# Who fetches the first token tiles, who splits the first expert's weights, and in which order the SyncE queue sees them

## The chip, the core and the metric

One NeuronCore of a Trainium2 chip runs the whole program in one launch. The metric is the device time of one execution in microseconds (us); lower is better. TensorE (PE, with its weight loads PEld), VectorE (DVE), ScalarE (ACT) and GpSimd (POOL) each run their own instruction stream in order. SyncE (SP) computes nothing: it issues DMAs, also in order, and reads a table entry into a register before a DMA whose address is only known at run time. POOL also issues DMAs, the indirect ones, whose row numbers lie in SBUF.

## The reference, cut to what matters

```python
# q, k, v: (8, 8, 576, 64) float32; 4608 tokens of 512 numbers come out of the attention
scores = scale * (q_c @ k_c.T)               # in chunks of 64 tokens, per batch and head
attn   = exp(scores - max); attn /= attn.sum(-1) + 1e-9
x      = (attn @ v_c)                        # -> (4608, 512)

logits     = norm(x) @ norm(expert_emb).T / tau       # 8 experts
expert_idx = argmax(logits);  gate_w = softmax(logits)[expert_idx]
for e in range(8):                                    # top-1 mixture, w1 (8,512,1024), w2 (8,1024,512)
    out[mask_e] = gate_w * (relu(x[mask_e] @ w1[e]) @ w2[e])

h = out @ w_in                                        # (512, 2048)
y = (h * sigmoid(1.702 * h)) @ w_out                  # (2048, 512)
```

## The kernel before, in words

The work has three stages. **Attention**: 36 tiles of 128 tokens (NTILE), one loop step `n` per tile plus three steps of tail. A step handles several tiles at different depths: scores of tile n (`emit_S`), probabilities of n-1, the product with V of n-2, and for tile n-3 `emit_X` (line 401), which makes a two-part f16 copy `xr` of the token rows (high part by DVE, low part by two POOL instructions, lines 417 and 418, for tiles below 33), and stores it to the DRAM table `xs`. `emit_XT` transposes `xr` on TensorE two to five steps later, ACT copies it out (`evac_XT`, line 437), and `emit_L` forms the router's logits.

**Routing**: after each batch of tiles the generator `gate` (line 504) works out on DVE, a few instructions at a time (`drip`, `steps`), each token's expert, weight and position; `place` (line 492) then scatters a tile's records into the DRAM tables `mtab[0]` and `mtab[1]` by an indirect POOL DMA. These wait in a list `scats` and are issued one or two a step by `scat`. After 24 tiles (NPART) the expert with most tokens is known; its first three tiles (NSURE) are taken from these 24, so that they can start before the attention ends. `first_load` (line 802) brings that expert's weights in eight SyncE DMAs of 512 KB, one a step from n = 31; `first_split` (line 813) cuts them into two f16 parts, sixteen pieces c = 0 to 15, two a step: ACT makes the high part, and the low part is made by DVE (one instruction) for even c and by POOL (two instructions, lines 788 and 789) for odd c. After the last batch, `tables` (line 642) works out where all later tiles lie (`idx_g`) and which expert weights come next.

**Mixture**: each tile i goes through `find(i)` (line 848: the tile's 128 records out of both halves of `mtab`; an indirect POOL DMA for i < 3, a SyncE DMA at a row read into a register for later ones), `fetch(i)` (line 860: POOL adds the halves and gathers the token rows from `xs` by an indirect DMA into `xg`, two buffers), `turn(i)` (line 876: a transposing SyncE DMA into `xTm`, two buffers), `mm1(i)` (line 893, 96 matmuls), and `mm2(i)` (line 926, 24 matmuls, then an evacuation that ends in a SyncE store to `ys`). mm1 of the first two tiles and the rest of the routing are interleaved by hand at lines 1049 to 1090. Then the next expert's weights are loaded (`load_next`, four DMAs of 1 MB), three blocks of the last stage's weights (`big_load`, 512 KB each) follow, and the loop at line 1266 runs over tiles 3 to 38: mm1(i), turn(i+2), fetch(i+3), find(i+4), a conditional swap of weights, mm2(i-1).

The last stage, a dense feed-forward network, starts when the loop ends and is not touched.

Of the kernel before, what the change touches and what calls it, by code (L numbers as in the profile page):

```python
# [17 lines left out]
ENG = mybir.EngineType  # L18
# [16 lines left out]
def kernel(  # L35
# [13 lines left out]
    nc = tc.nc  # L49
    B, H, S, D = q.shape  # L50
    NT, DM = out.shape
    NE = emb.shape[0]
# [451 lines left out]
    def gate(bi):  # L504
        t0, n = batches[bi]
        T = slice(t0, t0 + n)
        lg = lg_t.pop(bi)
        dl = small("dl", n, w=NE)
        nc.vector.tensor_copy(dl, lg[:, 0:n, NE:2 * NE])
        yield  # L510
        l = small("l", n, w=NE)
        nc.vector.tensor_tensor(out=l, in0=lg[:, 0:n, 0:NE], in1=dl, op=ALU.add)
        yield
        nc.vector.tensor_tensor(
            out=l, in0=l, in1=rn_all[:, T].unsqueeze(2).to_broadcast([128, n, NE]), op=ALU.mult
        )
        yield
        mx = small("mx", n)
        nc.vector.tensor_reduce(out=mx.unsqueeze(2), in_=l, axis=AX.X, op=ALU.max)
        yield  # L520
        nc.vector.tensor_tensor(
            out=l, in0=l, in1=mx.unsqueeze(2).to_broadcast([128, n, NE]), op=ALU.subtract
        )
        yield
        w = small("w", n, w=NE)
        nc.vector.scalar_tensor_tensor(
            out=w, in0=l, scalar=0.0, in1=io_re.unsqueeze(1).to_broadcast([128, n, NE]),
            op0=ALU.is_ge, op1=ALU.mult,
        )
        yield  # L530
        mw = small("mw", n)
        nc.vector.tensor_reduce(out=mw.unsqueeze(2), in_=w, axis=AX.X, op=ALU.max)
        yield
        oh = att.tile([128, 8, NE], F16, tag="g_oh", name="g_oh", bufs=2)[:, 0:n]
        nc.vector.tensor_tensor(
            out=oh, in0=w, in1=mw.unsqueeze(2).to_broadcast([128, n, NE]), op=ALU.is_equal
        )
        yield
        ex = small("ex", n, w=NE)
        nc.scalar.activation(out=ex, in_=l, func=AF.Exp)  # L540
        yield "pe"
        rkf = gb[:, 128:128 + n * NE]
        rk = rkf.rearrange("p (a e) -> p a e", a=n)
        ohf = oh.rearrange("p a e -> p (a e)")
        nc.tensor.matmul(rkf, tri16, ohf, start=True, stop=False)
        for j in range(1, n):
            nc.tensor.matmul(rkf[:, j * NE:], ones16, ohf[:, 0:(n - j) * NE], start=False, stop=False)
        nc.tensor.matmul(
            rk, ones16, cum.unsqueeze(1).to_broadcast([128, n, NE]), start=False, stop=True
        )  # L550
        sm = small("sm", NE)
        nc.vector.tensor_reduce(
            out=sm.unsqueeze(2), in_=oh.rearrange("p a e -> p e a"), axis=AX.X, op=ALU.add
        )
        yield
        nc.vector.tensor_tensor(out=cum, in0=cum, in1=sm, op=ALU.add)
        yield
        last = totals("cnt") if t0 + n in (NPART, NTILE) else None
        se = small("se", n)
        nc.vector.tensor_reduce(out=se.unsqueeze(2), in_=ex, axis=AX.X, op=ALU.add)  # L560
        yield
        nc.vector.tensor_scalar(se, se, 1e-9, None, op0=ALU.add)
        yield
        nc.vector.reciprocal(out=se, in_=se)
        yield
        nc.vector.scalar_tensor_tensor(
            out=meta[:, T, 0], in0=se, scalar=2.0 ** (-2 * W_EXP), in1=is_all[:, T],
            op0=ALU.mult, op1=ALU.mult,
        )
        yield  # L570
        po = small("po", n, w=NE)
        nc.vector.tensor_tensor(out=po, in0=rk, in1=oh, op=ALU.mult)
        yield
        pf = small("pf", n)
        nc.vector.tensor_reduce(out=pf.unsqueeze(2), in_=po, axis=AX.X, op=ALU.add)
        yield
        nc.vector.tensor_copy(pi_all[:, T], pf)
        yield
        scats.extend((now[0], lambda t=t: place(t)) for t in range(t0, t0 + n))
        if t0 + n == NPART:  # L580
            yield from order(last)
            first_weights()
            scats.extend((now[0], lambda i=i: find(i)) for i in range(NSURE))
            scats.extend((now[0], lambda i=i: fetch(i)) for i in range(2))
        if t0 + n == NTILE:
            yield from tables(last)

# [173 lines left out]
    def reg(ap, engines, hi):  # L761
        return nc.values_load(ap, engines=engines, min_val=0, max_val=hi)
# [50 lines left out]
    def first_split(n):  # L813
        for _ in range(n):
            c = fs_n[0]
            fs_n[0] += 1
            w_split(c // 8 + 1, c % 8, 512, (nc.vector, nc.gpsimd)[c % 2])

    flag = {}

# [26 lines left out]

    def find(i):
        mt_t[i] = [mo.tile([128, 2], F32, tag=f"mt{a}", name=f"mt{a}", bufs=6) for a in range(2)]
        row = reg(idx_g[0:1, i:i + 1], [ENG.SP], NE * NT - 128) if NSURE <= i < SURE else None  # L850
        for a in range(2):
            if row is not None:
                nc.sync.dma_start(out=mt_t[i][a][:, :], in_=mtab[a][bass.ds(row, 128), :])
                continue
            nc.gpsimd.indirect_dma_start(
                out=mt_t[i][a][:, :], out_offset=None, in_=mtab[a][:, :],
                in_offset=bass.IndirectOffsetOnAxis(ap=idx_g[:, i:i + 1], axis=0),
            )

    def fetch(i):  # L860
        mt, other = mt_t[i]
        nc.gpsimd.tensor_tensor(
            out=mt.bitcast(I32), in0=mt.bitcast(I32), in1=other.bitcast(I32), op=ALU.add
        )
        mt_t[i] = mt
        xg = mo.tile([128, 2 * DM], F16, tag="xg", name="xg", bufs=2)
        src = xs[0:NPART * 128, :] if i < NSURE else xs[:, :]
        nc.gpsimd.indirect_dma_start(
            out=xg[:, :], out_offset=None, in_=src,
            in_offset=bass.IndirectOffsetOnAxis(ap=mt_t[i].bitcast(I32)[:, 1:2], axis=0),  # L870
        )
        xg_t[i] = xg

    def turn(i):
        xT = mo.tile([128, 2 * KD, 128], F16, tag="xTm", name="xTm", bufs=2)
        nc.sync.dma_start_transpose(xT, xg_t.pop(i))
        xTm_t[i] = xT
# [34 lines left out]
    def mm2(i):  # L912
        mm2_part(i, 0, KF)
        mm2_evac(i)
# [89 lines left out]
    for n in range(NTILE + 3):  # L1004
        now[0] = n
        u, step = n // QR + 1, n % QR
        ev = [[], []]
        if u < NQ:
            ev = emit_T(u, "ku" if step == 0 else "qu")
            if step == 1 and u + 2 < NQ:  # L1010
                load_qk(u + 2)
        for f in ev[0]:
            f()
        on(n - 3, emit_sq)
        for f in ev[1]:
            f()
        turned = []
        if n - 1 in back:
            evac_XT(back[n - 1])
            turned.append(back[n - 1])  # L1020
        scat()
        drip(1)
        if n in front:
            emit_XT(front[n])
        on(n, emit_S, max_S)
        if n in front:
            evac_XT(front[n])
            turned.append(front[n])
        drip(1)
        on(n - 3, end_X)  # L1030
        drip(1)
        on(n - 1, emit_PT, evac_PT)
        on(n - 2, emit_PV)
        issue_v(v_due(n))
        if len(scats) > (4 if n < 30 else 0):
            scat()
        on(n, exp_S)
        drip(1)
        on(n - 2, emit_x)
        drip(1)  # L1040
        if n in back:
            emit_XT(back[n])
        for t in sorted(turned):
            end_L(t)
        if n >= NTILE - 5 and fl_n[0] < 8:
            while not first:
                drip(1)
            first_load()
        if n >= NTILE - 3:
            first_split(2)  # L1050
        if n == NTILE - 2:
            turn(0)
        if n == NTILE - 1:
            turn(1)
            fetch(2)
        if n >= NTILE:
            drip(6)
            mm1_part(0, n - NTILE)
# [19 lines left out]
        scat()  # L1078
    mm1_part(1, 3)
    steps(99)  # L1080
    find(3)
    mm2(0)
    mm1(2)
    fetch(3)
    turn(3)
    find(4)
    while todo:
        steps(1)
    fetch(4)
    att_stack.close()  # L1090


# [31 lines left out]
    def big_split():  # L1124
# [123 lines left out]
        run(99)  # L1248
        write()

    load_next(NSURE - 1, 1)
    load_next(NSURE - 1, 2)
    find(5)
    swap(NSURE, 1)
    mm2(1)
    turn(4)
    fetch(5)
    find(6)
    for b in range(NRAW):
        big_load(b)  # L1260
# [5 lines left out]
    for i in range(NSURE, SURE):  # L1266
# [6 lines left out]
            find(i + 4)  # L1273
        if i + 1 < SURE:
            swap(i + 1, 1)
        mm2_part(i - 1, 0, KF)
        swap(i, 2)
        mm2_evac(i - 1)
        if i < LASTD:
            next(dec, None)  # L1280
        if i == LASTD:
# [404 lines left out]
```

## Time and profile before

| What | Value |
|---|---|
| median of 3 executions | 1436.17 us (1432.81 to 1441.11) |
| the profiled execution | 1442.98 us, of which span 1441.2 us |
| TensorE busy | 1263.9 us (88% of the span) |
| VectorE, ScalarE, GpSimd busy | 1034.0 (72%), 721.1 (50%), 759.7 us (53%) |
| attention, TensorE's last score product | starts at 220.35 us |
| first mixture matmul | 240.48 us |
| mixture ends, last stage begins | about 720 us |

The span is cut into stages by the lines that run in it. A timeline row gives the start, the duration, the engine, the source line, what is written and read, and how often; brackets at its end hold the idle time ahead of it and what ended that idle time. Shares of busy time over the whole span say little here, since the change touches only the passage from attention to mixture, some 125 us long.

### The profile page before, as it was taken

The numbers are of one execution on the slowest core, as the hardware profiler recorded it, in microseconds if no ns is written. First come the engines' busy times: TensorE is split into PE (matmuls) and PEld (weight loads), VectorE is DVE, ScalarE is ACT, GpSimd is POOL, SyncE is SP. The second block draws the span as 40 slices with busy tenths as digits, with TensorE's granted clock in tenths as the row PEclk, the third lists the DMA queues.
The fourth block names the chain that finished last, engine by engine and source line by source line (L and its number), as shares of the span: only waits on it lengthen the run. The fifth ranks groups of instructions, "written<-read, shape, count | busy, mean of one in ns | idle before, by whom it ended". The sixth has DMA issues, their size and how long they took to land. (4 is left out here: it accounts for less than half of the span.)

```text
span 1441.2 us, 35556 instructions
## 1 busy us (share of the span) xinstructions
PE 1263.9 (88%) x14098; PEld 1043.1 (72%) x14098; DVE 1034.0 (72%) x1888; ACT 721.1 (50%) x1285; POOL 759.7 (53%) x676
## 2 busy tenths in 40 slices
PE   6767664779999999999879999998989999999995
PEld 4656553556766666676568888887878888888885
DVE  3868786826776668876568687877769696968681
ACT  6967653214453535553445464545454544545451
POOL 1445548413344344445037666666657575757663
PEclk8987975989999999999979999999999999999998
DMA  9888875175886768896604435351606262534412
GB/s 208 221 169 181 161 125 147 46 226 135 231 219 125 200 155 220 258 258 189 199 9 118 147 89 176 69 188 37 220 16 190 75 170 95 133 131 117 147 60 88
DMA packets 231224, 214.33 MB, mean 149 GB/s; under 512 B 139064, under 2 KB 184120, under 8 KB 231040
## 3 DMA queue, kind: packets, MB, share of 16 engines
q1 hardware_dynamic: 216304, 184.84, 49.8%
q0 software_dynamic: 7344, 19.71, 4.3%
q10 hardware_dynamic: 7392, 7.36, 1.6%
q8 instruction: 112, 1.84, 0.6%
q14 instruction: 72, 0.59, 0.2%
HBM read 155.06 MB, written 37.14 MB: 133 GB/s over the span
## 5 line engine op out<-in xcount | busy, mean ns | idle before, releaser
L1426 PEld LDWEIGHTS <-wS 128*128 128x128 f16 x3024 | 299.4, 99 | 73.1 <-issue 35.4
L893 PE MATMUL ph<-xTm,w1HL 128*128 128x128 f16 x3744 | 230.1, 225 | 35.5 <-DMA xTm<-xg 13.3
L893 PEld LDWEIGHTS <-w1HL 128*128 128x128 f16 x3744 | 222.6, 101 | 50.8 <-issue 14.9
L926 PE MATMUL py<-w2HL,hT 128*128 128x512 f16 x936 | 208.2, 379 | 0.0
L926 PEld LDWEIGHTS <-hT 128*128 128x128 f16 x936 | 90.1, 98 | 101.4
L1426 PEld LDWEIGHTS <-w2HL 128*128 128x128 f16 x864 | 84.5, 98 | 10.6
L1426 PEld LDWEIGHTS <-w1HL 128*128 128x128 f16 x864 | 84.6, 98 | 9.8
L1131 POOL TENSOR_TENSOR wS<-d_f,wS 128x512 f16<-128x512 f32 x28 | 35.9, 1283 | 95.0 <-ACT wS L1130 95.0
L1572 POOL DMA_INDIRECT out_dram<-hT,idc x36 | 36.4, 1011 | 94.0 <-DMA out_dram<-hT,idc 27.0
L1361 DVE TENSOR_TENSOR zA<-zA 128x512 f32<-128x512 f32 x72 | 73.5, 1021 | 16.4 <-POOL w2HL L1368 15.1
L1450 ACT ACTIVATE zA<-zA 128x512 f32<-128x512 f32 x72 | 44.5, 627 | 63.4 <-DVE zA L1447 35.7
L901 DVE SCALAR_TENSOR_TENSOR hT<-ph,hT 128x512 f16<-128x512 f32 x78 | 50.7, 682 | 34.6 <-ACT hT L900 33.9
L417 POOL TENSOR_TENSOR x<-x,sx_all 128x512 f32<-128x512 f32 x33 | 34.4, 1041 | 77.8 <-DVE rd L387 37.0
L939 ACT ACTIVATE ysq<-py 128x512 f16<-128x512 f32 x39 | 23.1, 593 | 93.8 <-PE py L926 78.3
L900 ACT ACTIVATE hT<-ph 128x512 f16<-128x512 f32 x78 | 44.1, 589 | 47.4 <-PE ph L893 45.4
L1368 POOL TENSOR_TENSOR w1HL<-zA,w1HL 128x512 f16<-128x512 f32 x36 | 51.1, 1419 | 23.6 <-ACT w1HL L1364 23.2
L952 ACT ACTIVATE y<-py,ysc 128x512 f16<-128x512 f32 x39 | 26.8, 687 | 72.2 <-DVE ysc L949 72.2
L341 DVE TENSOR_REDUCE mx<-sp 128x8 f32<-128x512 f32 x36 | 24.8, 689 | 51.2 <-PE sp L334 51.0
L494 POOL DMA_INDIRECT mtab<-meta,pi_all x36 | 37.2, 1033 | 43.5 <-DMA mtab<-meta,pi_all 16.9
L1426 PE MATMUL pb<-stg,wS 128*128 128x256 f16 x456 | 56.1, 276 | 3.9 <-ACT stg L1364 1.9
L312 ACT ACTIVATE kuT<-tp 64x512 f32<-64x512 f32 x72 | 45.2, 628 | 16.4 <-PE tp L307 15.4
L1426 PE MATMUL pa<-stg,wS 128*128 128x256 f16 x432 | 51.6, 273 | 1.9 <-ACT stgB L1364 1.9
(371 smaller groups left out, 3189.4 us busy)
## 6 DMA issues: line engine op xcount, KB each, us to landing
ring<-wod SPq DMA_DIRECT2D x63, 1024.0 KB
stg<-in_moe_w_dram SPq DMA_DIRECT2D x14, 1024.0 KB
stgB<-in_moe_w_dram SPq DMA_DIRECT2D x14, 1024.0 KB
ys<-y SPq DMA_DIRECT2D x39, 258.0 KB
vt<-in_v_dram SPq DMA_DIRECT2D x64, 144.0 KB
xs<-xr SPq DMA_DIRECT2D x36, 256.0 KB
raw_o<-in_moe_w_in_dram SPq DMA_DIRECT2D x16, 512.0 KB
raw_o<-in_moe_w_out_dram SPq DMA_DIRECT2D x16, 512.0 KB
```

The source lines that it names most:

```text
L312: lambda r=r, p=p, dst=dst: nc.scalar.activation(out=dst[:, :, r], in_=p[r * 64:(r + 1) * 64], func=AF.Copy)
L494: nc.gpsimd.indirect_dma_start(out=mtab[t % 2][:, :], out_offset=bass.IndirectOffsetOnAxis(ap=pi_all[:, t:t + 1], axis=0), in_=meta[:, t, ...
L893: nc.tensor.matmul(p[:, f % 4], wt[:, c, fs], xT[:, a, :], start=(c == 0 and a == 0 and wt is w1H), stop=(c == KD - 1 and wt is w1L),)
L900: nc.scalar.activation(out=hi, in_=p, func=AF.Relu)
L901: nc.vector.scalar_tensor_tensor(out=lo, in0=p, scalar=0.0, in1=hi, op0=ALU.max, op1=ALU.subtract)
L926: nc.tensor.matmul(p, hT[:, a, :], wt[:, c, :], start=st, stop=sp)
L1131: nc.gpsimd.tensor_tensor(out=L_, in0=f, in1=H_, op=ALU.subtract)
L1361: nc.vector.tensor_tensor(out=o, in0=x, in1=p, op=op)
L1368: eng.tensor_tensor(out=lo, in0=x, in1=hi, op=ALU.subtract)
L1426: nc.tensor.matmul(dst, lhs(a, k, ab), rhs(b, k), start=first and ab == 0 and k == 0 and m == 0, stop=(k == n - 1 and m == 2), skip_group_ ...
L1450: nc.scalar.activation(out=z, in_=z, func=AF.Sigmoid, scale=1.702 * 2.0 ** -G_EXP)
L1572: nc.gpsimd.indirect_dma_start(out=out[:, :], out_offset=bass.IndirectOffsetOnAxis(ap=id_t[j][0][:, 2 * h + t, 0:1], axis=0), in_=o_t[j, h ...
```

## The change

Finds of tiles 0 to 2 go from POOL to SyncE, and are issued together at the end of step n = 32, after all waiting scatters; fetch(0) and fetch(1) leave the list and stand at fixed steps (n = 33 and n = 34). All sixteen low parts of the first weights are made by DVE. find(3), find(4) and find(5) are issued together before mm2(0), and fetch(4) follows fetch(3) at once. mm2(1), mm2(2), turn(4) and fetch(5) now stand ahead of the loads of the next expert's weights; mm2(2) ran inside the loop, after mm1(3), before.

```diff
@@ gate
             first_weights()
-            scats.extend((now[0], lambda i=i: find(i)) for i in range(NSURE))
-            scats.extend((now[0], lambda i=i: fetch(i)) for i in range(2))
@@ first_split
-            w_split(c // 8 + 1, c % 8, 512, (nc.vector, nc.gpsimd)[c % 2])
+            w_split(c // 8 + 1, c % 8, 512, nc.vector)
@@ find
-        row = reg(idx_g[0:1, i:i + 1], [ENG.SP], NE * NT - 128) if NSURE <= i < SURE else None
+        row = reg(idx_g[0:1, i:i + 1], [ENG.SP], NE * NT - 128) if i < SURE else None
@@ the attention loop, end of a step
         if n >= NTILE - 3:
             first_split(2)
+        if n == NTILE - 4:
+            while scats:
+                scat()
+            for i in range(NSURE):
+                find(i)
+        if n == NTILE - 3:
+            fetch(0)
         if n == NTILE - 2:
+            fetch(1)
             turn(0)
@@ after the attention
     steps(99)
-    find(3)
+    for i in range(3, 6):
+        find(i)
     mm2(0)
     mm1(2)
     fetch(3)
+    fetch(4)
     turn(3)
-    find(4)
     while todo:
         steps(1)
-    fetch(4)
@@ ahead of the mixture loop
+    mm2(1)
+    mm2(2)
+    turn(4)
+    fetch(5)
     load_next(NSURE - 1, 1)
     load_next(NSURE - 1, 2)
-    find(5)
     swap(NSURE, 1)
-    mm2(1)
-    turn(4)
-    fetch(5)
     find(6)
     for b in range(NRAW):
         big_load(b)
@@ in the mixture loop
-        mm2_part(i - 1, 0, KF)
+        if i > NSURE:
+            mm2_part(i - 1, 0, KF)
         swap(i, 2)
-        mm2_evac(i - 1)
+        if i > NSURE:
+            mm2_evac(i - 1)
```

## Rows read from the trace of the kernel before

**Rows 1.** Busy time by stretch; last three columns: granted clock, DMA share, GB/s

```profile
214.00:240.00 26.00, 9.06 (x140) 7.27 (x141) 13.92 (x41) 9.12 (x16) 21.23 (x23) 0.50 0.41 117
292.00:307.00 15.00, 10.41 (x106) 7.33 (x103) 3.05 (x10) 2.57 (x5) 1.17 (x2) 0.96 1.05 323
```

**Rows 2.** Timeline of POOL, end of the attention: start, duration, line, idle before

```profile
212.76 0.98 POOL L855 DMA_INDIRECT mt<-mtab,idx_g  x1 [8.58 <-DMA mtab<-meta,pi_all]
216.49 0.96 POOL L855 DMA_INDIRECT mt<-mtab,idx_g  x1 [2.74 <-DMA mtab<-meta,pi_all]
...
222.16 1.05 POOL L788 TENSOR_TENSOR stg<-stg,w_pow 128x512 f32<-128x512 f32 x1
...
229.59 1.05 POOL L868 DMA_INDIRECT xg<-xs,mt  x1 [0.27 <-POOL mt L862]
```

**Rows 3.** Waits of 195 to 335 us: waiter, releaser, us in total, times, longest

```profile
PE sp L431 <- POOL xr L418: 15.5, 3, 5.8
```

**Rows 4.** Timeline of SP, two of the loads of the first weights

```profile
203.56 0.34 SPq L808 DMA_DIRECT2D stg<-in_moe_w_dram  x1
...
220.30 0.34 SPq L808 DMA_DIRECT2D stg<-in_moe_w_dram  x1
```

**Rows 5.** Timeline of ACT, end of the attention

```profile
216.06 1.15 ACT L786 ACTIVATE w1HL<-stg 128x512 f16<-128x512 f32 x2 [2.77 <-DMA stg<-in_moe_w_dram]
...
224.98 1.15 ACT L786 ACTIVATE w1HL<-stg 128x512 f16<-128x512 f32 x2
...
237.42 1.02 ACT L437 ACTIVATE xTa<-sp 128x1024 f16<-128x1024 f16 x1 [6.53 <-PE sp L431]
```

**Rows 6.** Timeline of DVE, routing

```profile
242.13 0.19 DVE L521 TENSOR_TENSOR g_l<-g_l,g_mx 128x32 f32<-128x32 f32 x1
...
242.84 1.64 DVE L535 TENSOR_TENSOR g_oh<-g_w,g_mw 128x32 f16<-128x32 f32 x1
...
248.00 0.68 DVE L791 SCALAR_TENSOR_TENSOR w2HL<-stg,w2HL 128x512 f16<-128x512 f32 x1
...
265.71 1.63 DVE L556 TENSOR_TENSOR cum<-cum,g_sm 128x8 f16<-128x8 f16 x1
```

**Rows 7.** Timeline of PE, routing and first mixture tiles

```profile
240.48 2.27 PE L893 MATMUL ph<-xTm,w1HL 128*128 128x128 f16 x24
...
264.34 0.18 PE L545 MATMUL gb<-g_oh,tri 128*128 128x32 f16 x1 [3.42 <-DVE g_oh L535]
...
267.39 0.17 PE L603 MATMUL gb<-cum,ones 128*128 128x8 f16 x1 [1.43 <-DVE cum L556]
...
290.27 6.97 PE L893 MATMUL ph<-xTm,w1HL 128*128 128x128 f16 x96 [5.59 <-DMA xTm<-xg]
...
309.83 7.40 PE L893 MATMUL ph<-xTm,w1HL 128*128 128x128 f16 x96 [7.42 <-DMA xTm<-xg]
...
322.25 5.52 PE L893 MATMUL ph<-xTm,w1HL 128*128 128x128 f16 x96
327.61 5.34 PE L926 MATMUL py<-w2HL,hT 128*128 128x512 f16 x24
```

**Rows 8.** Timeline of SP, first mixture tiles

```profile
287.11 1.27 SPq L876 DMA_TRANSPOSE xTm<-xg  x1
289.73 0.89 SPq L853 DMA_DIRECT2D mt<-mtab  x2
292.18 1.04 SPq L768 DMA_DIRECT2D stg<-in_moe_w_dram  x2
...
295.86 2.00 SPq L853 DMA_DIRECT2D mt<-mtab  x2
...
301.88 2.83 SPq L876 DMA_TRANSPOSE xTm<-xg  x1
```

**Rows 9.** Timeline of POOL, the addition ahead of fetch(5)

```profile
308.54 0.19 POOL L862 TENSOR_TENSOR mt<-mt,mt 128x2 int32<-128x2 int32 x1 [14.81 <-DMA mt<-mtab]
```

**Rows 10.** Timeline of DVE, last step of the evacuation of mm2(2)

```profile
304.71 0.75 DVE L953 SCALAR_TENSOR_TENSOR y<-py,ysc,y 128x512 f16<-128x512 f32 x1 [0.76 <-ACT y L952]
```

## Prediction

> **What bounds the kernel now.** I read the busy time by stretches first, to find where TensorE is not the bound, then each engine's timeline there, and at each gap asked which engine's instruction ended it. The mixture loop and the last stage are close to solid on TensorE (88% of the span by the page), so what counts is when the loop gets going. Between the last attention tiles and the sixth mixture tile it is not solid: from 214 to 240 us TensorE works 9.06 of 26 us at a granted clock of 0.50 (its lower level, 1.2 GHz), while POOL works 21.23 [rows 1]. Three passages lose time.
>
> Passage A, 204 to 240 us, belongs to POOL. The two DMAs of find(0) wait there for scattered records to land, until 212.76 and 216.49 [rows 2]; the low half of a tile's token rows queues behind them, and TensorE's transposes wait for it, three times, 15.5 us in all [rows 3]. The odd weight pieces (two POOL instructions each, the first 1.05 us [rows 2]) stand in the same queue. So the first mixture matmul starts at 240.48 [rows 7].
>
> Passage B, 240 to 268 us, belongs to the DVE chain of the router. Small DVE instructions that take 0.19 us take up to 1.64 where a POOL half of a weight piece runs beside them; five on the chain do so, the first at 242.84, the last at 265.71, with an excess of 1.45 + 0.85 + 1.43 + 0.98 + 1.46 = 6.2 us [rows 6]. TensorE waits for this chain 3.42 and 1.43 us [rows 7].
>
> Passage C, 284 to 328 us, belongs to the transposing DMAs: TensorE waits 5.59 us for tile 3 and 7.42 us for tile 4, and the mm1 after each runs 6.97 and 7.40 us instead of 5.52 [rows 7]. The second wait has 4 MB of weights in front of it on the SP queue: these are issued from 292.18 and turn(4) at 301.88 [rows 8].
>
> **A, part by part.** The six finds leave POOL, and so do the eight odd pieces. The wait for the scatter's landing doesn't go: SP now holds it, at the end of step 32, and behind it stand the store of tile 30 and the third weight load, while POOL's fetch(0) waits for find(0) at the end of step 33. SP: the second half of find(0) is issued when POOL's was, 216.49, and takes until 216.9. A later find costs a register read (288.38 to 289.73 = 1.35) and two issues (0.89), 2.24 us [rows 8]; two of them end at 221.4. The store and the load add 0.5, so the third load is issued at 221.9, against 220.30 before [rows 4]: 1.6 us later. Its landing takes at most 4.7 us by the split that followed without a wait at 224.98, but the second load, issued at 203.56, was waited for until 216.06, 12.5 us [rows 4, 5]. I take 4, since the DMA engines have little to do in this stretch (share 0.41 [rows 1]), and keep both ends. ACT then splits pieces 4 and 5 from 225.9 (1.15), does a square (0.7 at most), copies out tile 31 (1.02), waits 0.7 for TensorE to transpose tile 32, and copies out tile 32 from 229.5. Before, that copy ran at 237.42 [rows 5]. POOL doesn't hold it: fetch(0) follows the landing of find(0) at about 219.3, ends at 220.8, and the low halves of tiles 31 and 32, two instructions of like size each, with fetch(1) between, end by 227. The token rows of tile 0 are then fetched 9.8 us sooner than at 229.59 [rows 2]. So the tail gains 7.9 us; I take A = 7.5, with ends 0 (a 12.5 us landing) and 9.5 (POOL alone the limit).
>
> **B.** The five stretched instructions lose their neighbour: 2.3 us of excess on the way to tile 34's transposes, 3.9 on the way to TensorE's two waits. DVE gets eight pieces more at 0.68 us [rows 6]; the first three lie in A, where DVE waits for others, piece 7 and piece 13 lie on the chain, the other three beside waits for mm1. So 2.3 - 0.7 = 1.6 and 3.9 - 0.7 = 3.2; the second is less than the 4.85 us that TensorE waits [rows 7]. B = 4.8; ends -1 (no relief, all five late pieces partly on the chain) and 6.2.
>
> The Trainium skill has a rule here that speaks against a part of it ("SBUF — State Buffer", "Who interferes with whom"): an instruction of VectorE with two SBUF inputs and a GpSimd instruction that reads SBUF exclude each other, and whichever was issued first holds the other up. The moved pieces are such instructions, so they may now hold up POOL's low halves of tiles 31 and 32. By that rule A would lose up to two pieces, 1.4 us, and the sum with it; the stretched rows 6 agree with it in the other direction, and no row shows this one.
>
> **C.** Times in this part are on the old clock, to be shifted by A + B. mm2(1) ends at 284.68 (290.27 less 5.59). mm2(2) now follows, 5.34, to 290.02, so tile 3's transposed rows, there at 290.27 before and sooner now, stop no one: mm1(3) runs 5.52 to 295.5. find(4) and find(5) ahead of ys(0) cost SP 2 x 2.24 = 4.5 us, which lie inside its wait for xg(3) until 287.11 [rows 8]; without that cover they would cost up to 4.5. turn(4) stands behind the store of mm2(2). That evacuation took 3.05 us (302.41 to 305.46) [rows 7, 10], so the store is issued at 293.1 and turn(4) at 293.6; landing takes 3.16 (287.11 to 290.27), mm1(4) starts at 296.8, a wait of 1.3, and mm2(3) ends at 307.7.
>
> What is late next is tile 5. Its rows are gathered early, but turn(5) comes after load_next and big_load on SP. The first weight load is issued at 293.6 + 1.27 + 1.56 (the gap ahead of 292.18) = 296.5, and 4.19 + 1.57 = 5.77 MB are queued ahead of turn(5), which SP issues near 305. That a small transfer waits for the big ones ahead of it is seen in find(5): 1 KB, issued at 295.86 behind the weights, was waited for until 308.54 [rows 8, 9]. At 323 GB/s [rows 1] the queue takes 17.9 us, to 314.4, and the transposes 3.2 more: mm1(5) starts at 317.6 after a wait of 9.9 us. After so long a wait I give it the 7.40 us of tile 4, and it ends at 325.0, against 327.6 to 327.8 before [rows 7]. C = 2.6. So this passage mostly moves its second wait one tile on.
>
> The Trainium skill ("DMA: Bandwidth & Descriptors", "Queues, rings and completion order") says that the write which reports a DMA's end lands only after every earlier write of that DMA engine, in whichever queue. By that rule the case below in which tile 5 goes free has no chance; rows 9 agree with it.
>
> **The sum.** 7.5 + 4.8 + 2.6 = 14.9 us of the profiled execution's 1442.98, so 1428.1; that execution lies 0.5% above the median of 1436.17, on which the same share gives 1421.3. I let the gain stand to the end, since TensorE, as said, bounds most of what follows.
>
> **Rivals.**
> - *Tile 5 goes free* (turn(5) isn't held by the loads): mm1(5) starts at 307.7 and ends at 313.2, C = 14.4, sum 26.7, 1409.6. For it: SP issues turn(5) before TensorE needs it by 2 us. Against: rows 9. Chance 0.17.
> - *The tail gains nothing*: the third weight load lands as slowly as the second (12.5 us), ACT stands still until 234.4 and copies out tile 32 at 238.0. A = 0, the sum is 7.4, 1428.8. For it: SP's order, and that the scatter's landing stays on the path. Against: by 222 the DMA engines are no longer loaded. Chance 0.17.
> - *Slower*: the 5.77 MB ahead of turn(5) move slowly, and the wait at tile 5 eats A and B. It decides from where mm1(5) ends 12.3 us later than before, at 339.9: 32.8 us for the queue, 176 GB/s. At the 117 GB/s of 214 to 240 us [rows 1] it is 49.3 us, mm1(5) ends at 356.4, and the sum is 16.5 us lost, 1452.6. Against: that stretch had little queued, and the weights moved at 323. Chance 0.12.
>
> **How the numbers follow.** The forecast, 1421.3 (1414 to 1429 by its own), has 0.49; 0.05 is left for what I don't see. About 0.5% (7.2 us) is what a measurement can tell from no change. Faster takes the forecast, the free tile and 0.06 of the second rival, 0.72; within 0.5% takes the rest of it, 0.05 of the slow queue and 0.02, 0.18; slower takes 0.07 of the slow queue and 0.03, 0.10. The range, 1406 to 1438, holds the first two rivals and leaves out the slow queue.
>
> **What would show it.** A: no transposes waiting 5 us for xr; ACT waiting for the third load near 222 to 226; first mm1 near 233. B: router instructions of 0.2 us throughout; waits near 264 down to about 1 us together. C: no wait at tile 3, about 1 at tile 4, about 10 at tile 5, ended by the transposing DMA. The forecast is wrong if the first mm1 isn't at least 4 us sooner, or if tile 5 starts less than 2 us or more than 15 us after mm2(3) ends.

## The result and the profile after

The changed kernel took 1429.2 us (median of 20 runs, 1418.86 to 1437.64) against 1441.24 for the kernel before beside it (20 runs): a ratio of 0.9917, 95% interval 0.9892 to 0.9943, that is 12.0 us, between 8.2 and 15.6. The forecast was 14.9 us off the profiled execution, 1.03% against 0.83% measured. The profiled execution took 1424.5 us with a span of 1422.8.

To place the gain I cut the trace at five instructions of TensorE: the scores of the fourth attention tile from the end (*S*), the first mixture matmul, mm2(0), mm2(4) and the first matmul of the last stage. A is the first stretch, B the second, C the third, D the fourth. Before, S stands at 194.94 us, and A, B, C, D last 45.54, 28.28, 58.85 and 394.10 us; after, S stands at 198.53 and they last 35.85, 23.25, 56.32 and 393.86. So A gives 9.7 us, B 5.0, C 2.5, together 17.3; by a second execution of the changed kernel (e12 below) they give 11.4, 4.4 and 0.5, together 16.3. The spans differ by 18.4: S comes 3.6 us later and the last stage is 4.5 us shorter, in code that the change doesn't touch. Nothing of the three gains is lost again in D.

The same two stretches by busy time, as in [rows 1]; the second is the one in which the weights move. The last columns are the granted clock, the DMA share and GB/s.

```profile
214.00:240.00 26.00, 16.07 (x295) 13.94 (x295) 22.82 (x77) 13.43 (x27) 11.19 (x12) 0.65 0.74 177
285.00:304.00 19.00, 15.12 (x182) 11.69 (x179) 1.93 (x4) 2.00 (x4) 1.16 (x2) 0.95 1.11 331
```

TensorE now works 16.07 of the 26 us, POOL 11.19 instead of 21.23, and VectorE, with 22.82, has taken POOL's place as the engine that is nearly full.

**Passage A** in order of time, all engines (start, duration, engine, line, operation, and in brackets the idle time ahead and what ended it):

```profile
210.47 10.73 SPq L851 DMA_DIRECT2D mt<-mtab  x6
...
219.15 0.19 POOL L860 TENSOR_TENSOR mt<-mt,mt 128x2 int32<-128x2 int32 x1 [8.02 <-DMA mt<-mtab]
...
220.31 3.74 DVE L789 SCALAR_TENSOR_TENSOR w1HL<-stg,w1HL 128x512 f16<-128x512 f32 x2
...
220.88 1.05 POOL L417 TENSOR_TENSOR x<-x,sx_all 128x512 f32<-128x512 f32 x1
...
221.89 0.33 SPq L806 DMA_DIRECT2D stg<-in_moe_w_dram  x1
222.01 1.49 POOL L418 TENSOR_TENSOR xr<-x,xr 128x512 f16<-128x512 f32 x1
...
225.54 1.02 ACT L437 ACTIVATE xTa<-sp 128x1024 f16<-128x1024 f16 x1 [4.41 <-DVE g_pf L575]
...
226.62 1.01 PE L431 MATMUL sp<-ident,xr 128*128 128x128 f16 x8 [3.88 <-ACT xTa L437]
...
227.46 1.15 ACT L784 ACTIVATE w1HL<-stg 128x512 f16<-128x512 f32 x2
...
228.69 1.28 DVE L789 SCALAR_TENSOR_TENSOR w1HL<-stg,w1HL 128x512 f16<-128x512 f32 x2
...
230.21 1.01 PE L431 MATMUL sp<-ident,xr 128*128 128x128 f16 x8 [2.39 <-ACT xTa L437]
...
231.32 1.02 ACT L437 ACTIVATE xTa<-sp 128x1024 f16<-128x1024 f16 x1 [1.16 <-PE sp L431]
...
234.38 1.97 PE L891 MATMUL ph<-xTm,w1HL 128*128 128x128 f16 x24
```

The six finds now hold SP for 10.73 us, and POOL's fetch(0) waits 8.02 us for their landing. Behind it a tile's low half (220.88 to 223.5) runs beside two weight pieces (2 and 3) on VectorE, and these take 3.74 us, where two take 1.28 at 228.69. The router's DVE instructions stand behind them, ScalarE waits 4.41 us for one of those, TensorE 3.88 us for ScalarE. No transpose waits for POOL's `xr` any more, which before cost 15.5 us [rows 3]. The copy that stood at 237.42 in [rows 5] stands at 231.32, and as before the first mixture matmul follows it by 3.06 us.

**Passages B and C** on TensorE, beside [rows 7]:

```profile
253.78 0.18 PE L545 MATMUL gb<-g_oh,tri 128*128 128x32 f16 x1 [0.96 <-DVE g_oh L535]
...
256.27 0.17 PE L601 MATMUL gb<-cum,ones 128*128 128x8 f16 x1 [0.86 <-DVE cum L556]
...
257.63 5.34 PE L924 MATMUL py<-w2HL,hT 128*128 128x512 f16 x24
...
281.76 7.47 PE L891 MATMUL ph<-xTm,w1HL 128*128 128x128 f16 x96 [2.90 <-ACTq L838]
290.10 0.28 PE L891 MATMUL ph<-xTm,w1HL 128*128 128x128 f16 x2 [0.87 <-ACTq L838]
...
306.19 0.37 PE L891 MATMUL ph<-xTm,w1HL 128*128 128x128 f16 x2 [4.88 <-DMA xTm<-xg]
307.08 7.03 PE L891 MATMUL ph<-xTm,w1HL 128*128 128x128 f16 x94 [0.51 <-DVEq L838]
313.95 5.34 PE L924 MATMUL py<-w2HL,hT 128*128 128x512 f16 x24
```

The waits for the router fall from 3.42 and 1.43 to 0.96 and 0.86 us. In C tile 3 waits 2.90 us for ScalarE, tile 4 0.87 for the same, tile 5 4.88 for its transposing DMA. "ACTq L838" is ScalarE's sequencer at the conditional weight swap. Tile 3's wait isn't always that one: in e12, the same kernel once more, TensorE waits there for the transposing DMA.

```profile
291.13 6.83 PE L891 MATMUL ph<-xTm,w1HL 128*128 128x128 f16 x96 [4.79 <-DMA xTm<-xg]
```

What ScalarE and SP did meanwhile in the changed kernel, one fence each, and then what SP itself waited for at the raw blocks (L1125) and at turn(5) (L874; us in total, times, longest):

```profile
280.44 0.69 ACT L950 ACTIVATE y<-py,ysc 128x512 f16<-128x512 f32 x1 [0.79 <-DVE ysc L947]
...
302.73 0.66 ACT L1142 ACTIVATE d_t<-raw_o 128x512 f32<-128x512 f32 x1 [12.86 <-DMA raw_o<-in_moe_w_in_dram]
```

```profile
282.48 1.30 SPq L874 DMA_TRANSPOSE xTm<-xg  x1
286.30 1.02 SPq L766 DMA_DIRECT2D stg<-in_moe_w_dram  x2
...
292.54 6.38 SPq L1125 DMA_DIRECT2D raw_o<-in_moe_w_in_dram  x3
301.27 1.30 SPq L874 DMA_TRANSPOSE xTm<-xg  x1
```

```profile
SPq L1125 <- DMA stgB<-in_moe_w_dram: 3.8, 1, 3.8
SPq L874 <- DMA stgB<-in_moe_w_dram: 2.2, 1, 2.2
SPq L1125 <- DMA stg<-in_moe_w_dram: 1.5, 1, 1.5
```

The eviction of mm2(2) ends on ScalarE at 281.13, and tile 3 starts right behind it. turn(5) is issued at 301.27, behind the loads, and not only behind them in order: SP stands until the expert's weights (`stg`, `stgB`) have landed, 1.5 and 3.8 us between the raw blocks and 2.2 us ahead of turn(5). And ScalarE stands 12.86 us at the first raw block of the last stage's weights, until 302.73: a second wait beside the one that TensorE shows. It bears on the experiments below.

### The profile page after: what moved, and what is told of

It is laid out like the page before. It is cut to its first block, busy times and chain, and to the rows that moved or that the text cites. A ratio compares the mean times of both kernels' runs of the same rounds, so it can differ in the third digit from the quotient of the medians.

```text
span 1422.8 us, 35560 instructions
## 1 busy us (share of the span) xinstructions
PE 1263.0 (89%) x14098; PEld 1043.1 (73%) x14098; DVE 1029.2 (72%) x1896; ACT 721.9 (51%) x1285; POOL 738.5 (52%) x654
## 5 line engine op out<-in xcount | busy, mean ns | idle before, releaser
L891 PEld LDWEIGHTS <-w1HL 128*128 128x128 f16 x3744 | 221.7, 101 | 47.2 <-ACTq L838 15.6
L312 ACT ACTIVATE quT<-tp 64x512 f32<-64x512 f32 x72 | 45.3, 630 | 16.4 <-PE tp L307 15.5
L1434 PE MATMUL pd<-stg,wS 128*128 128x256 f16 x432 | 51.7, 272 | 1.9 <-ACT stgB L1372 1.9
## 6 DMA issues: line engine op xcount, KB each, us to landing
raw_o<-in_moe_w_in_dram SPq DMA_DIRECT2D x16, 512.0 KB
raw_o<-in_moe_w_out_dram SPq DMA_DIRECT2D x16, 512.0 KB
```

The lines of the kernel that those rows point to most:

```text
L312: lambda r=r, p=p, dst=dst: nc.scalar.activation(out=dst[:, :, r], in_=p[r * 64:(r + 1) * 64], func=AF.Copy)
L891: nc.tensor.matmul(p[:, f % 4], wt[:, c, fs], xT[:, a, :], start=(c == 0 and a == 0 and wt is w1H), stop=(c == KD - 1 and wt is w1L),)
L1434: nc.tensor.matmul(dst, lhs(a, k, ab), rhs(b, k), start=first and ab == 0 and k == 0 and m == 0, stop=(k == n - 1 and m == 2), skip_group_ ...
```

## The experiments

All are edits of the changed kernel. The table gives the stretches of the profiled execution (us), their sum, and the ratio of times to the kernel before, each measured beside runs of it.

| kernel | A | B | C | D | sum | ratio, 95% interval |
|---|---|---|---|---|---|---|
| before | 45.54 | 28.28 | 58.85 | 394.10 | 526.8 | 1 |
| changed | 35.85 | 23.25 | 56.32 | 393.86 | 509.3 | 0.9917 (0.9892 to 0.9943) |
| e1_find_pool | 38.97 | 23.58 | 55.38 | 397.10 | 515.0 | 0.9895 (0.9862 to 0.9927) |
| e2_split_pool | 36.52 | 27.88 | 55.75 | 396.72 | 516.9 | 0.9971 (0.9946 to 0.9996) |
| e3_old_order | 35.26 | 23.49 | 61.47 | 397.37 | 517.6 | 0.9946 (0.9913 to 0.9978) |
| e4_low_dve | 36.98 | 27.02 | 55.87 | 394.08 | 513.9 | 0.9935 (0.9909 to 0.9961) |
| e5_swap_first | 36.11 | 24.85 | 54.26 | 396.98 | 512.2 | 0.9899 (0.9864 to 0.9933) |
| e6_blocks_late | 34.71 | 25.03 | 57.58 | 395.14 | 512.5 | 0.9889 (0.9831 to 0.9948) |
| e7_loads_late | 34.16 | 24.44 | 61.45 | 397.33 | 517.4 | 0.9941 (0.9908 to 0.9974) |
| e8_loads_decode_late | 35.17 | 23.40 | 51.02 | 400.25 | 509.8 | 0.9935 (0.9900 to 0.9969) |
| e9_all_late | 34.27 | 24.09 | 46.27 | 407.16 | 511.8 | 0.9933 (0.9902 to 0.9964) |
| e10_decode_late | 35.42 | 24.59 | 55.32 | 401.64 | 517.0 | 0.9954 (0.9924 to 0.9984) |
| e11_catch_up | 36.48 | 27.53 | 47.08 | 402.58 | 513.7 | 0.9903 (0.9868 to 0.9938) |
| e12_changed_again | 34.17 | 23.89 | 58.35 | 395.57 | 512.0 | 0.9902 (0.9866 to 0.9938) |

The last row is the changed kernel once more, measured anew beside e11: its stretches move by 0.6 to 2.0 us from one execution to the next. They can move by more: e5 to e11 run the changed kernel's code up to mm2(0) too, and over these seven executions and the two of the changed kernel, nine in all, A lies between 34.2 and 36.5 and B between 23.3 and 27.5; e8 and e11 have the same code through C too, with 51.02 and 47.08. Differences of that size are not read from a stretch alone.

**Which half of passage A: the finds (e1, e2).** e1 puts the finds of tiles 0 to 2 and the first two fetches back on POOL, and keeps the split:

```diff
+            scats.extend((now[0], lambda i=i: find(i)) for i in range(NSURE))
+            scats.extend((now[0], lambda i=i: fetch(i)) for i in range(2))
-        if n == NTILE - 4: ... find(i) for tiles 0 to 2
-        if n == NTILE - 3: fetch(0)
-            fetch(1)
```

> The changed kernel with the finds of tiles 0 to 2 and the fetches of tiles 0 and 1 back on POOL's list; all else as changed. Three stretches are read from the trace: A from the scores of tile 32 to the first mixture matmul (45.5 us before, 35.9 after), B from there to mm2(0) (28.3, 23.3), C from there to mm2(4) (58.9, 56.3). Theory (the finds held POOL's queue, and the weight pieces held it too): POOL waits for the scatter again until the place of tile 23 has landed, so low halves come late, but no weight pieces queue behind them: A about 41, B and C as after (23, 56); time about 5 us above the changed kernel, ratio to before about 0.995. Rival 1 (only the weight pieces mattered): A stays near 36, ratio as after, 0.992. Rival 2 (only the finds mattered): A back at 45, ratio about 0.999.

e2 puts the odd weight pieces back on POOL, and keeps the finds on SP:

```diff
-            w_split(c // 8 + 1, c % 8, 512, nc.vector)
+            w_split(c // 8 + 1, c % 8, 512, (nc.vector, nc.gpsimd)[c % 2])
```

> The changed kernel with the odd pieces of the first weights back on POOL; all else as changed. Theory (the odd pieces stretch the router's DVE instructions and delay TensorE's two waits): B back to about 28, small DVE instructions of the router up to 1.6 us again; A within 2 us of 35.9, since the third and fourth piece on DVE now cost a stretch of their own (3.74 us for two instead of 1.29); C as after. Ratio to before about 0.995. Rival (B's gain came from the earlier start and its clock, not from the neighbour on POOL): B stays near 23, ratio 0.992.

In e1 the time is rival 1's and A lies between theory and rival 1; e2 came out as its theory has it. Either half alone gives most of A: 38.97 with the split alone, 36.52 with the finds alone, 35.85 with both, 45.54 with neither. It took both loads on POOL's queue to make the low halves late; with one gone, the other fits, and in neither e1 nor e2 does a transpose wait for `xr`. In e1 the scatter's landing still holds POOL:

```profile
215.23 0.96 POOL L855 DMA_INDIRECT mt<-mtab,idx_g  x1 [5.30 <-DMA mtab<-meta,pi_all]
216.22 1.05 POOL L417 TENSOR_TENSOR x<-x,sx_all 128x512 f32<-128x512 f32 x1
```

but the low half follows at once, with no weight piece between. So the finds' move to SP added no time that can be measured on top of the split (0.9895 without it). The split acts on B as well: with the pieces back on POOL (e2) B is 27.88, only just above the nine executions, but these VectorE instructions of the router are stretched again, each beside a POOL instruction of a piece (POOL runs these from 255.40 and from 264.60):

```profile
254.90 1.58 DVE L210 SCALAR_TENSOR_TENSOR g_a<-rn_all,ss_all 128x4 f32<-128x4 f32 x1
...
264.82 0.95 DVE L556 TENSOR_TENSOR cum<-cum,g_sm 128x8 f16<-128x8 f16 x1
```

e2 is the only version whose interval stands apart from e1's: the move of the eight pieces is the one part of the change whose worth the time shows by itself.

**The order of C undone (e3).** Finds, fetch(4) and mm2(2) where they were before:

```diff
-    for i in range(3, 6):
-        find(i)
+    find(3)
...
-    mm2(1)
-    mm2(2)
-    turn(4)
-    fetch(5)
     load_next(NSURE - 1, 1)
     load_next(NSURE - 1, 2)
+    find(5)
     swap(NSURE, 1)
+    mm2(1)
+    turn(4)
+    fetch(5)
```

> The changed kernel with the order after the attention as before (find(4), find(5), fetch(4), mm2(1), mm2(2), turn(4), fetch(5) in their old places behind the loads); the tail of the attention as changed. Theory (moving tiles 4 and 5 ahead of the weights only moves the wait from tile 4 to tile 5): A and B as after (36, 23), C back to about 59, with waits of about 5 us at tile 3 and 7 at tile 4 and none at tile 5; 2 to 3 us slower than the changed kernel, ratio to before about 0.994. Rival (the order is worth its two waits): C about 66 to 70, ratio about 1.0.

```profile
276.34 6.84 PE L891 MATMUL ph<-xTm,w1HL 128*128 128x128 f16 x96 [8.91 <-DMA xTm<-xg]
...
294.87 7.77 PE L891 MATMUL ph<-xTm,w1HL 128*128 128x128 f16 x96 [6.51 <-DMA xTm<-xg]
```

With the old order C is 61.47, longer than before the change by 2.6: TensorE comes sooner, tile 3's rows don't, and its wait grows from the 5.59 us of [rows 7] to 8.91. Beside A and B the new order is worth 5.2 us in the trace (3.1 against e12), more than C shrank by; the time (0.9946) doesn't resolve it.

**The halves of tiles 31 and 32 on VectorE (e4).**

```diff
-        if t < LATE:
+        if t < 31:
             nc.gpsimd.tensor_tensor(out=xf, in0=xf, in1=sx.to_broadcast([128, DM]), op=ALU.mult)
```

> The changed kernel with the low halves of tiles 31 and 32 made by one DVE instruction each instead of two on POOL. In the changed kernel the pieces 2 and 3 took 3.74 us on DVE beside two such POOL instructions, 1.29 elsewhere, and the next row maximum waited for them. Theory (what bounds the tail now is DVE held up by POOL's instructions): the two pieces take 1.3 us, A falls by about 2.4 us to 33.5; ratio to before about 0.990. Rival (the tail is bound by the landing of the third weight load or by the SP queue): A stays at 35.9 within 0.5, ratio as after, 0.992.

A doesn't fall: it is 36.98, where the changed code has 34.2 to 36.5. Without POOL's tensor instructions beside them two pieces do take 1.29 us again, but ScalarE, which splits ahead of VectorE, now waits 1.45 us for the third weight load:

```profile
224.75 1.15 ACT L784 ACTIVATE w1HL<-stg 128x512 f16<-128x512 f32 x2 [1.45 <-DMA stg<-in_moe_w_dram]
```

```profile
225.41 1.29 DVE L789 SCALAR_TENSOR_TENSOR w1HL<-stg,w1HL 128x512 f16<-128x512 f32 x2 [1.12 <-ACT w1HL L784]
```

So the rival has it in kind: with VectorE freed, the landing of that load is the next bound. TensorE also stood 2.93 us in the middle of a tile's scores in this execution, for nothing that the profile shows, so a gain smaller than that isn't excluded. B, 27.02, lies within the nine executions, and the time (0.9935) shows no gain.

**The wait at tile 3 (e5).** The swap for tile 3 goes ahead of the eviction of mm2(2):

```diff
-    mm2(2)
+    mm2_part(2, 0, KF)
     turn(4)
...
     swap(NSURE, 1)
+    mm2_evac(2)
```

> The changed kernel with the evacuation of mm2(2) placed behind the conditional swap of tile 3 on ACT and DVE; turn(4), fetch(5) and the loads thus no longer stand behind the store of tile 2. In the changed kernel mm1(3) waited 2.9 us for ACT's branch of that swap and then ran 7.47 us instead of 5.52. Theory (the start of mm1(5) is set by the DMA queue ahead of turn(5), so what is won at tile 3 is waited for again at tile 5, and only the earlier issue of the loads, about 2.6 us, counts): no wait at tile 3, a longer one at tile 5 (about 7), C (from mm2(0) to mm2(4)) 53.7 instead of 56.3; about 2.6 us faster than the changed kernel. Rival (the wait at tile 3 counts in full): C 51 or less.

```profile
272.83 5.52 PE L891 MATMUL ph<-xTm,w1HL 128*128 128x128 f16 x96 [1.05 <-DMA xTm<-xg]
...
296.75 0.37 PE L891 MATMUL ph<-xTm,w1HL 128*128 128x128 f16 x2 [6.32 <-DMA xTm<-xg]
```

Tile 3 no longer waits for ScalarE but 1.05 us for its transposes, so the swap alone wasn't its bound. It ends 3.8 us sooner after mm2(0) than in the changed kernel, and tile 5 waits 6.32 instead of 4.88: C keeps 2.1 us of the 3.8, and the rest is waited for at the queue, as the theory has it.

**What tile 5 waits for (e6, e7, e10).** e6 issues the three raw blocks behind turn(5), e7 the expert weights as well (which holds only where tile 3 belongs to the first expert, as it does in these inputs):

```diff
-    load_next(NSURE - 1, 1)   (e7 alone)
-    load_next(NSURE - 1, 2)   (e7 alone)
-    for b in range(NRAW):
-        big_load(b)
...
             turn(i + 2)
+        if i == NSURE:   the same loads here (in e7 behind fetch(i + 3))
```

> The changed kernel with the three blocks of the last stage's weights (1.57 MB) loaded behind turn(5) instead of ahead of it. Theory (turn(5) waits for the bytes queued ahead of it on SP): at 336 GB/s these are 4.7 us; the wait of 4.88 us at tile 5 all but goes, mm1(5) runs 5.5 us instead of 7.0, C 50 to 52 instead of 56.3, about 5 us faster. Rival (turn(5) waits for the expert's weights alone, or for its place in SP's program): the wait stays, C 55 to 57, same time.

> The changed kernel with the next expert's weights (4 MB) and the three blocks loaded behind turn(5) and fetch(6) in the first pass of the mixture loop; it holds only where tile 3 belongs to the first expert, as here. Theory (these loads are what tile 5 waits for): no wait for a transposing DMA at tiles 3 to 5, C 50 (56.3 less 4.9 of wait and 1.5 of slow clock), and none at tile 6, whose rows should land near 311 where TensorE wants them at 313; about 6 us faster than the changed kernel. Rival (the wait moves on once more): a wait of 3 us or more at tile 6 or 7, the time as the changed kernel's.

Neither came out in C. TensorE and ScalarE in e7:

```profile
309.87 0.39 PE L891 MATMUL ph<-xTm,w1HL 128*128 128x128 f16 x2 [9.27 <-ACTq L838]
```

```profile
307.00 0.66 ACT L1142 ACTIVATE d_t<-raw_o 128x512 f32<-128x512 f32 x1 [17.84 <-SPq L828]
```

The transposes are free, and tile 5 waits longer than ever, 9.27 us (5.11 in e6), now for ScalarE. The decode's first step on ScalarE waits for a raw block (the releaser in the row, SP's branch at L828, had itself waited for that block, which landed at 306.82), and in program order tile 4's relu and the swap for tile 5 stand behind it. Whatever makes that block land later makes tile 5 later. The DMA half of e6's theory did come out: turn(5)'s rows landed 44.2 us after mm2(0), where the changed kernel has 48.4. So my theory that the transposing DMA alone bounded tile 5 fell: there are two bounds less than 1 us apart. In the changed kernel ScalarE goes on at 302.73, mm1(5) starts at 306.19 by the DMA, and after two matmuls it waits 0.51 us more, until 307.08, for VectorE's side of the swap, which follows on ScalarE's relu.

e10 tests the pair from the other side: the decode one pass later, the loads unmoved.

```diff
-        if i < LASTD:
+        if NSURE < i < LASTD:
             next(dec, None)
```

> The changed kernel with the decode alone starting one pass later, the loads where they were. Theory: in the changed kernel the transposing DMA is the last bound of tile 5, ScalarE's is only some 0.5 us behind it; so the wait at tile 5 stays at 4.5 to 5 us and is ended by the DMA, the stretch is 55.5 to 56 us and the time is the changed kernel's (0.991). Rival: ScalarE was the bound and the DMA only named; the wait goes, the stretch is 51 to 52 us and the time some 4 us lower.

```profile
311.25 7.15 PE L891 MATMUL ph<-xTm,w1HL 128*128 128x128 f16 x96 [3.70 <-DMA xTm<-xg]
```

The theory held for the stretch, nearly: C 55.32, a wait of 3.70 us (4.5 to 5 expected) ended by the DMA. Taking away either bound alone shows no gain beyond the spread between the two executions of the changed kernel (56.32 and 58.35), and e7 loses 3 to 5 us.

**Both bounds taken away (e8, e9).** e8 is e7 with e10's edit. e9 is that with e5's order, the expert weights behind turn(5) and the blocks a pass later, behind turn(6).

> As e7 (the fourth tile's gate, up and down weights and the first three blocks fetched one pass later, which holds only where the tile before belongs to the same expert), and the decode of the last stage's blocks starts one pass later. Theory: in e7 the transposing DMA no longer bound tile 5, ScalarE did, which stood in order at the first decode block (17.8 us for its data) with tile 4's relu and the conditional swap for tile 5 behind it. With the decode out of that place no wait over 1 us is left at tile 5, the stretch from mm2 of the first tile to mm2 of the fifth (56.3 us in the changed kernel, 61.5 in e7) is about 50 us, and the time is some 6 us below the changed kernel's, ratio about 0.988. Rival: the bound is the DMA traffic itself and it comes back as a DMA wait at tile 5 or as a wait at tile 6; the stretch stays at 56 us or more and the time is that of the changed kernel or above.

> e8 and e5 together: the swap for tile 3 ahead of the second layer's eviction of tile 2, the expert weights behind the fifth transposing DMA, the three blocks behind the sixth, the decode one pass later (holds only where tile 3 belongs to the first expert). Theory: the two bounds of tile 5 (transposing DMA, ScalarE at the decode) and the 2 us of tile 3 are all taken away; no wait over 1.2 us at tiles 3 to 5, stretch 45.5 to 48 us, some 8 to 10 us faster than the changed kernel, ratio about 0.985. Rival: the wait moves on to tile 6 or into the attention's last stage, where the blocks come later, and half or more of the gain is given back: ratio 0.990 or above.

In the trace the theory came out for tile 5: it waits for nothing, and C is 51.02 in e8 and 46.27 in e9, 5 and 10 us shorter than the changed kernel's 56.32. Tile 3 still waits for its transposes, 4.55 us in e8 and 2.42 in e9, where 1.2 at most was expected; and as e8's code has C at 47.08 in e11, what e9 adds to it isn't shown. The time didn't follow: 0.9935 and 0.9933. In e9 the wait moves on to tile 6, which is behind the decode's block in the same way, and costs 2.97 + 1.20 us and a slow mm1 there:

```profile
308.32 0.28 PE L891 MATMUL ph<-xTm,w1HL 128*128 128x128 f16 x2 [2.97 <-ACTq L838]
309.80 6.82 PE L891 MATMUL ph<-xTm,w1HL 128*128 128x128 f16 x94 [1.20 <-DVEq L838]
```

The rest went 400 us further on. The longest wait of SP, then TensorE and VectorE of e8, end of the mixture:

```profile
SPq L1297 <- DMA wod<-sg: 9.0, 1, 9.0
```

```profile
705.84 0.61 PE L1396 MATMUL pa<-ysq,onesB 128*128 128x512 bf16 x1 [11.30 <-DVE ysq L1389]
```

```profile
702.24 0.17 DVE L939 COPY y<-mt 128x2 int32<-128x2 int32 x1 [9.71 <-DMA ys<-y]
```

Ahead of the last stage TensorE stands 11.30 us instead of the changed kernel's 4.31, since VectorE waits 9.71 us (2.00 there) for the store of the last tile's first half to free its buffer. A decode begun a pass later ends a pass later; the last decoded weights are written later, the last stage's loads wait 9.0 us for them on SP (no such wait in the changed kernel), and the store stands behind these. e9 and e10 have the same wait, and TensorE stands 11.90 and 11.52 us. So in e10 D is 6 to 8 us longer, more than C could have gained; in the time (0.9954) a loss against the changed kernel isn't shown.

**The decode caught up (e11, e12).** e8 with one extra step of the decode in the eleventh pass; and the changed kernel itself beside it.

```diff
         if NSURE < i < LASTD:
             next(dec, None)
+        if i == NSURE + 10:
+            next(dec, None)
```

> e8 with one more step of the decode in the eleventh pass of the loop, so that the decode ends as early as in the changed kernel (holds only where tile 3 belongs to the first expert). Theory: e8's 5 us at tile 5 were given back at the end of the mixture, where the last decoded weights were written one pass later, the last stage's first loads waited for them and the last tile's result waited behind these (PE idle 11.3 us ahead of the last stage, 4.3 in the changed kernel). With the decode caught up the idle is 4 to 5 us again, the time some 6 us below e8's and 4 below the changed kernel's: ratio about 0.988 to 0.989. Rival: the extra step takes back its price in its own pass (some 4 us of VectorE), or the idle ahead of the last stage stays: ratio 0.992 to 0.994.

> The changed kernel itself, unaltered, on the chip of e11 and beside it. Theory: the ratio to the kernel before is 0.9917 within its interval, and e11 is 3 to 5 us faster. Rival: chips or occasions differ by more than the experiments do, and the changed kernel comes out as fast as e11.

The idle time went as expected:

```profile
710.46 0.61 PE L1398 MATMUL pa<-ysq,onesB 128*128 128x512 bf16 x1 [4.31 <-DVE ysq L1391]
```

But D stayed long, 402.58, mostly since tile 6 waits for its transposes (3.32 us and a 7.15 us mm1, 5.0 us together), and the passes around the extra step have waits at the swap that the changed kernel doesn't have. The time is that of the changed kernel beside it, 0.9903 against 0.9902. e12's rival held; e11's ratio lies between its theory and its rival. No version tried here is shown to be faster than the changed kernel.

## Why the prediction was right, and where not

**The sum.** 14.9 us forecast; 12.0 measured by time, with 14.9 inside the interval, and 17.3 in the profiled pair. A was under-sized (7.5 forecast, 9.7, with e12's 11.4 beside it). B (4.8, 5.0) and C (2.6, 2.5) came out by size in this one pair, which is partly luck: e12 has 4.4 and 0.5, and the changed kernel's B is the shortest of nine executions, whose middle one (24.44) would give 3.8. That the gain stands to the end held: D is 394.10 before and 393.86 after (395.57 in e12).

**A: the third weight load.** Issued at 221.89, forecast 221.9; but the match is luck. S stands 3.6 us later in this execution, so against S the load was issued 3.6 us sooner than I had it, as SP was done with the finds sooner. It landed at 227.31, 5.4 us after its issue where I took 4; the net 2.2 us are what A was under-sized by. The split of pieces 4 and 5 began at 227.46 and the copy of tile 32 followed it by 3.9 us, 3.6 in my working.

What I didn't have is a second bound just as late. ScalarE did stand from 221.1 to 225.54, in the stretch that I named for the load, yet for VectorE; and what I had put down as free, "the first three lie in A, where DVE waits for others", wasn't: two pieces took 3.74 us beside POOL's low half. That this was the binding part isn't shown. The load landed 0.15 us before the split, e4 frees VectorE and finds ScalarE waiting for the load, and over the nine executions the two pieces take from 1.74 to 3.74 us without A following.

The Trainium skill ("SBUF — State Buffer", "Who interferes with whom") foretold it in kind: an instruction of VectorE with two SBUF inputs and a GpSimd instruction that reads SBUF take the shared port in turns. I weighed it as a loss of up to 1.4 us for POOL. The trace has it mostly on VectorE: 3.74 - 1.28 = 2.5 us, while POOL's L418 took 1.49 where it takes 1.16 at 227.59. e4 agrees (1.29 us with POOL silent). By the rule A would have lost up to 1.4 us; no loss shows in it.

**A: the parts.** The prediction gave the finds and the pieces one answer. Apart, they turned out to overlap almost wholly (e1, e2). The rival that the tail gains nothing fell: the scatter's landing does stay on the path (8.02 us of POOL, 10.73 of SP), and a low half still stands behind fetch(0), but the transposes no longer wait for the low halves.

**B.** Right in mechanism: the router's VectorE instructions take 0.13 to 0.22 us again, and e2 brings the stretched ones back. The size, as said, is between 0.8 and 5.0 by execution.

**C: tile 3.** "No wait at tile 3" failed by 2.90 us and a mm1 of 7.47 instead of 5.52, and for two reasons. I followed SP's queue past mm2(2) and not ScalarE's: its eviction stands there ahead of the conditional swap for tile 3, and mm1(3) waits for that branch (e5 takes it away). I had the row for it, since the eviction's 3 us are in the prediction, used for the store alone. And tile 3's rows, which I had as "sooner now", came later: they landed 23.6 us after mm2(0) began (25.9 in e12), against 21.5 before the change, and TensorE was free for them at 21.2. Why isn't shown; SP stands 4.85 us at the finds of tiles 3 to 5 ahead of turn(3), which I had put down as covered.

**C: tile 5.** That tile 5 follows the loads held: by my working mm1(5) starts 48.84 us after mm2(0), and it started 48.56 after it (49.54 in e12). As TensorE came 4.7 us later than I had it, its wait was 4.88 us and not 9.9, and the error at tile 3 doesn't show in C. A step inside failed: I had SP issue turn(5) 36 us after mm2(0), and the transposes wait 9.4 us in the queue. SP issued it at 43.6, when the last of the expert's weights had landed, and the rows landed 4.8 us later, behind the raw blocks. The queue's speed, 323 GB/s in the forecast, is 331 in the row above, which removes the slow-queue rival. That tile 5 goes free is also out as long as turn(5) stands behind the loads; put ahead of them (e8, e9), it does go free.

The Trainium skill ("DMA: Bandwidth & Descriptors", "Queues, rings and completion order") had given that rival no chance, and the trace agrees, though no run here tells its rule from plain order on the queue. What I had not seen either is SP's own wait for the weights, and ScalarE's wait for the raw block as a second bound, nearly as late.

## What to carry to other kernels

When an instruction moves, follow the queue of every engine that takes part in it, ScalarE's conditional branches and evictions too, and not just the queue that you moved it for. Two loads on one queue that are together too much don't add up as two gains: price each with the other gone. And before you take away a wait, look for engines that stand idle until nearly the same moment: here two bounds lay 0.15 us apart at the third load, 0.6 at tile 3 and less than 1 at tile 5, and once both were gone at tile 5 the 5 to 10 us came back as waits one tile on and at the far end of the loop.

## What the runs showed of the hardware

Two VectorE pieces (128x512, two SBUF inputs) took 3.74 us beside a pair of POOL tensor instructions and 1.28 us without (1.74 to 3.54 in the other executions of the same code); POOL's own second instruction grew from 1.16 to 1.49. The three issues of the raw blocks, together 1.57 MB, held SP for 6.38 us, of which the profile puts 5.3 down to the landing of weights issued before them; they held it for 2.92 in e7 and 1.32 in e9, where they come later. A transposing DMA issued with 4.19 MB of weights ahead of it landed 9.5 us after its issue, 1.1 us after the weights (e6), and 3.1 us after its issue with none of these loads ahead of it (e7). Executions of the same code spread widely before the change's place: S stands between 189.57 (e5) and 207.09 us (e12), and the last stage, untouched in all versions, lasts 709.2 (e1) to 724.7 us (e11). Against that spread, and with intervals of some 4 to 5 us to either side, a gain of 5 us in a stretch of the trace can go unseen in the time.
